# Pooled attention and a two-layer network on one core: the first four pairs of heads take fp32 products from TensorE

## The chip, the core and the metric

The kernel runs on one core of a Trainium2 chip. Five engines run side by side, each in the order of its own program: TensorE (PE, with its weight loads as PEld), VectorE (DVE), ScalarE (ACT), GpSimd (POOL) and SyncE (SP), which issues the DMAs. [...] The metric is the device time of one execution in microseconds; the profile's span runs from the first to the last instruction of one profiled execution.

## The reference

```python
q_pool = q.reshape(B, H, S // 2, 2, D).mean(axis=3)      # B, H, S, D = 4, 8, 1152, 64
scores = (1 / sqrt(D)) * q_pool @ k.T                      # 576 x 1152 per head
attn   = softmax(scores)                                   # over the 1152 keys
x      = (attn @ v) -> rows of 8 heads x 64 = 512          # 2304 rows
out    = (relu(x @ w_in) ** 2) @ w_out                     # 512 -> 2048 -> 512
```

All inputs and the output are fp32.

## The kernel before

Heads are worked on in 16 pairs, four for each batch. For a pair, `prep` loads K, Q and V (`LK`, `LQ`, `LV`), sums the two queries that are pooled (`QS`), finds a power of two as a scale for each (a maximum over sums of squares: ACT `Square` for pairs 0 and 5 to 15, TensorE products `GR` and `GM` for pairs 1 to 4, then the short chain `GF`, `GS`, `GT`, `GU`, `GW`), and splits each into two fp16 tensors, high and low (`KA`/`KD`, `QA`/`QD`, `VA`/`VD`). K and Q are then turned by DMA transposes (`KT`, `QT`), and `QX` copies the low half of Q to the other 64 partitions.

`chunk` handles 128 query rows, 9 chunks for a pair, 144 in all: scores `S` on TensorE (six fp16 matmuls), the row maximum `MX` on DVE, the exponential `EX` on ACT, which gives P in fp32. P goes on in one of two ways. Most chunks split it into high and low on ACT, POOL or DVE (`HI`, `LO`) and turn both by a DMA transpose (`TR`). The chunks of the list `TURNB` (16 of the first 36) are turned by TensorE: nine fp32 transposes in three groups (`TP`), each group in one of two PSUM banks, from which `TH` takes the high half and `TL` the rest. `group` then multiplies with V (`PV`): for each of 9 blocks of keys, three products (high by high, high by low, low by high) for each of two heads, whose 64 output rows lie beside each other, so 54 matmuls of 256 or 320 columns. `ED` scales the result into x.

`weights` brings in the two weight matrices in 16 pieces; each is taken apart and split by ACT, DVE and POOL (`W1` to `W5`, `WA`, `WB`, `WD`). `block` computes the network for 256 rows (9 blocks): after the sums (`RV`, `RB`, `XR`) and a split of x (`XA`, `XD`) come 192 matmuls `H` and 96 matmuls `O`, with `HA`, `G1`, `G2`, `G3` between. A block needs all four pairs of its batch, so the first `H` comes after the first four pairs; the other twelve pairs run between `H` and `O` of earlier blocks.

`add` only notes an operation with its engines' costs, what it depends on and the buffers it takes. `Plan.order` then lays all operations out in a model of the engines and takes, for an engine that comes free, the operation of smallest priority among those that can start soon; the priority is the position in the work plus an offset for the kind of operation (`CFG['off']`, and `off0` for the first part). What comes out is the order in which each engine's instructions are written. Two PSUM banks `a` serve `TP`, `PV`, `H`, `O` and the small products alike; the scores have two areas of three banks each, which become six banks `t` once the last scores are done.

Of the kernel before, what the change touches and what calls it, by code (L numbers as in the profile page):

```python
# [8 lines left out]
F32 = mybir.dt.float32  # L9
# [47 lines left out]
class Plan:  # L57
# [15 lines left out]
    def add(self, name, engs, deps, emit, at, take=None, give=None, after=()):  # L73

        kind = name[0]
        off, off0 = cfg("off", {}), cfg("off0", {})
        self.at[name] = len(self.ops)
        prio = cfg("nudge", {}).get(len(self.ops), 0.0) + at + off.get(kind, DEF.get(kind, 0.0)) + (off0.get(kind, 0.0) if at < self.early else 0.0)
        self.ops.append(
            dict(name=name, engs=dict(engs), deps=[d for d in deps if d], emit=emit, pos=at, prio=prio, take=take, give=give, after=after)  # L80
        )
# [120 lines left out]
ALT = {"W4": "D", "NP": "A", "ED": "D", "HI": "PD", "LO": "P", "KA": "P", "QA": "P", "QX": "P", "VA": "P", "XA": "", "WA": "", "WD": "", "HA": "D", "G2": "PD", "G3": "D", "XQ": "", "RU": "D"}  # L202
DEF = {
# [7 lines left out]
def kernel(  # L211
# [133 lines left out]

    def prep(n):
# [44 lines left out]
        qse = alt("QS", POOL=1400, DVE=640)  # L391
        if gram_:
# [14 lines left out]
            for i, nm in enumerate("kqv"):  # L407
                L = "L" + nm.upper()
                add(("GR", n, nm), {"PE": 560}, [(L, n)], lambda o, i=i, nm=nm: gram(o, i, nm), need, take=(("GR", n, nm), ("a",), 0))
                add(("GM", n, nm), {"DVE": 200}, [("GR", n, nm)], lambda o, i=i, nm=nm: gmax(o, i, nm), need, give=("GR", n, nm))  # L410
            add(("QS", n), qse, [("GR", n, "q")], qsum, need)
            fdep = [("GM", n, nm) for nm in "kqv"]
        else:
# [12 lines left out]
            add(("QS", n), qse, [("LQ", n)], qsum, need)  # L426
            add(("QK", n), {"ACT": 1200}, [("LK", n)], lambda o: sq(o, 0, "k"), need, take=ktake)
            add(("QV", n), {"ACT": 1200}, [("LV", n)] + oldv, lambda o: sq(o, 2, "v"), need)
            add(("QQ", n), {"ACT": 700}, [("QS", n)], lambda o: sq(o, 1, "q"), need, take=qtake)
# [40 lines left out]
        for w, i0, i1 in (("qk", 0, 2), ("v", 2, 3)):  # L470
            fd = [d for x, d in zip("kqv", fdep) if x in w]
# [48 lines left out]
        add(("KA", n), alt("KA", ACT=1170, POOL=1400), [("GW", n, "qk"), ("LK", n)] , ka, need, take=kt_)  # L520
        add(("KD", n), {"DVE": 1500}, [("KA", n)], kd, need, give=("k", n))
        add(("KT", n), {"SP": 3200}, [("KD", n)] + old, kt, need, give=("k2", n))
        add(("QA", n), alt("QA", ACT=600, POOL=700), [("GW", n, "qk"), ("QS", n)] , qa, need, take=qt_)
        add(("QD", n), {"DVE": 760}, [("QA", n)], qd, need, give=("q", n))
        add(("QT", n), {"SP": 1700}, [("QD", n)] + old, qt, need, give=("q2", n))
        add(("QX", n), alt("QX", DVE=1100, POOL=2500), [("QT", n)] + old, qx, need)
        add(("VA", n), alt("VA", ACT=1170, POOL=1400), [("GW", n, "v"), ("LV", n)] + oldv, va, need)
        add(("VD", n), {"DVE": 1480}, [("VA", n)], vd, need, give=("v", n))

    def done(c):  # L530
        if c in turned_b:
            return [("TL", c, x) for x in range(3)]
        return [("TL", c)] if c in turned else [("TR", c)]
# [6 lines left out]
    def chunk(i):  # L540
# [12 lines left out]
        def st3():  # L553
            return sts[i % 2].rearrange("p a b -> p (a b)")[:, :1152]

# [72 lines left out]
        ring = [("PV", v_, GR_[g_]) for v_, g_ in ring]  # L628
        if i in turned:
# [77 lines left out]
    def group(vi, r):  # L707
# [7 lines left out]
        def pv(o):  # L715
            vv = v2s[preps[n]["slot"]]
            px = bank(o)
            tl["px", vi, r] = px
            ps = [(vl, pl, kc) for vl, pl in ((1, 0), (0, 0), (0, 1)) for kc in range(NC)]
# [8 lines left out]
        def ed(o):  # L728
            px, sc = tl.pop(("px", vi, r)), tl["esc", n][:, 1:2]
# [4 lines left out]
        pc = 27 * (112 if N == TB else 138) + 100  # L734
# [3 lines left out]
        add(("PV", vi, r), {"PE": pc}, dn + [("VD", n)] + old, pv, last, take=(("PV", vi, r), ("a",), 0))  # L738
        add(("ED", vi, r), alt("ED", ACT=620 if r else 380, DVE=560 if r else 370), [("PV", vi, r), ("GE", n, "v")] + old,
# [397 lines left out]
    turned_b = {i for i in cfg("TURNB", range(0, FB, 4)) if CH[chunks[i][1]] is not None}  # L1137
# [12 lines left out]
    with tc.manual_schedule():  # L1150
# [7 lines left out]
        nc.vector.tensor_scalar(pick, pick, 2.0 ** -14, None, op0=ALU.mult)  # L1158
        for o in seq:
# [34 lines left out]
```

## Time and profile before

| what | value |
|---|---|
| time of three runs, median | 877.98 us (875.13 to 878.1) |
| span of the profiled execution | 873.5 us |
| what lies around the span, by the median | 4.5 us |
| busy in the span | PE 743.7, DVE 653.3, ACT 610.7, POOL 403.0 us |
| first matmul of the network (`H`) starts | 259.74 us |

The windows give busy microseconds and the granted TensorE clock of a stretch. A group of instructions lists the number, the busy time and the mean length in ns. In the timeline the first number is the start.

### The profile page before, as it was taken

How to read it: one execution, taken by the hardware profiler on the slowest of the kernel's cores; microseconds unless marked ns; L12 is line 12 of the kernel's file. 1: busy time of each engine (PE TensorE's matmuls, PEld its weight loads, DVE VectorE, ACT ScalarE, POOL GpSimd, SP SyncE). 2: the span in 40 equal slices, each digit the busy share in tenths (PEclk: the TensorE clock that was granted, in tenths of full speed). 3: DMA queues.
4: the chain of work that ended last, by engine and by line, in shares of the span. 5: the costliest groups of instructions: out<-in, count | busy, mean ns of one | idle time of the engine just before them, and what ended most of it. 6: DMA issues, size and time to landing. Idle time of an engine off the chain costs nothing. (4 is left out here: it accounts for less than half of the span.)

```text
span 873.5 us, 15476 instructions
## 1 busy us (share of the span) xinstructions
PE 743.7 (85%) x6041; PEld 495.6 (57%) x6041; DVE 653.3 (75%) x817; ACT 610.7 (70%) x959; POOL 403.0 (46%) x281
## 2 busy tenths in 40 slices
PE   0567656767579999998999999898999999999997
PEld 0344534544347567754775576566647756858573
DVE  4897999997878887988989788879788974312120
ACT  4666886778988778866896767777767984625150
POOL 2454436755878644555465266537835531100000
PEclk9976877799869999999999999999999999999999
DMA  7798796797668999989998989996889997000001
GB/s 220 223 176 210 163 245 179 184 220 150 134 144 156 174 160 201 164 182 184 173 195 150 197 159 172 204 179 141 153 183 181 183 158 133 2 13 13 13 14 24
DMA packets 346888, 133.39 MB, mean 153 GB/s; under 512 B 330176, under 2 KB 330176, under 8 KB 346816
## 3 DMA queue, kind: packets, MB, share of 16 engines
q1 hardware_dynamic: 346816, 132.41, 74.9%
q8 instruction: 47, 0.77, 0.4%
q14 instruction: 25, 0.20, 0.1%
HBM read 45.09 MB, written 4.72 MB: 57 GB/s over the span
## 5 line engine op out<-in xcount | busy, mean ns | idle before, releaser
L580 DVE TENSOR_REDUCE ca<-s 128x1 f32<-128x1152 f32 x144 | 192.6, 1348 | 13.5 <-PE s L572 8.9
L591 ACT ACTIVATE buf<-s,ca,esc 128x1152 f32<-128x1152 f32 x144 | 188.9, 1312 | 7.7 <-DMA PT<-buf 1.2
L603 POOL TENSOR_TENSOR buf<-buf,buf 128x1152 f16<-128x1152 f32 x60 | 152.6, 2545 | 88.2 <-ACT buf L595 61.9
L865 PEld LDWEIGHTS <-w 128*128 128x128 f16 x1728 | 168.7, 98 | 32.4 <-issue 8.3
L572 PE MATMUL s<-kT,qT 128*128 128x512 f16 (+1 forms) x768 | 156.9, 348 | 18.7 <-ACT buf L591 17.8
L914 PE MATMUL ba<-w,region 128*128 128x512 f16 x624 | 141.6, 379 | 0.7 <-DVE region L797 0.5
L914 PEld LDWEIGHTS <-region 128*128 128x128 f16 x864 | 82.9, 98 | 96.2 <-issue 2.9
L865 PE MATMUL ba<-region,w 128*128 128x256 f16 x1080 | 124.4, 274 | 6.3 <-DVE x L797 3.5
L572 PEld LDWEIGHTS <-qT 128*128 128x128 f16 x768 | 71.9, 105 | 86.1 <-issue 37.5
L723 PE MATMUL ba<-PT,v 128*64 128x256 f16 (+1 forms) x1728 | 116.0, 293 | 5.6 <-DVE PT L681 4.5
L723 PEld LDWEIGHTS <-v 128*64 128x64 f16 x1728 | 97.8, 113 | 22.5 <-issue 12.3
L603 DVE TENSOR_TENSOR buf<-buf,buf 128x1152 f16<-128x1152 f32 x56 | 84.6, 1510 | 14.6 <-ACT buf L595 12.3
L590 ACT ACTIVATE ca<-ca,cols,esc 128x1 f32<-128x1 f32 x144 | 54.6, 379 | 50.4 <-DVE ca L580 49.9
L892 DVE TENSOR_TENSOR region<-region 128x512 f16<-128x512 f32 x41 | 35.0, 854 | 63.0 <-ACT region L885 62.5
L658 PE MATMUL ba<-ident,buf 128*128 128x128 f32 x252 | 47.6, 312 | 35.2 <-DVE PT L681 14.7
L340 POOL TENSOR_SCALAR buf<-buf,cols 128x1152 f16<-128x1152 f32 x31 | 42.6, 1373 | 63.9 <-ACT buf L591 55.9
L595 ACT ACTIVATE buf<-buf 128x1152 f16<-128x1152 f32 x59 | 68.5, 1161 | 2.5 <-DVE buf L603 0.6
L343 DVE SCALAR_TENSOR_TENSOR buf<-raw,psc,buf 128x576 f16<-128x576 f32 x48 | 64.5, 1381 | 5.6 <-POOL buf L317 3.2
L658 PEld LDWEIGHTS ba<-ident,buf 128*128 128x128 f32 x252 | 31.3, 159 | 50.4 <-DVE PT L681 18.9
L892 POOL TENSOR_TENSOR region<-region 128x512 f16<-128x512 f32 x31 | 43.7, 1411 | 32.4 <-ACT region L885 29.5
L667 ACT ACTIVATE PT<-ba 128x384 f16<-128x384 f32 x84 | 39.2, 485 | 20.0 <-PE ba L658 19.4
L914 PE MATMUL bt<-w,region 128*128 128x512 f16 x240 | 52.9, 379 | 0.0
(135 smaller groups left out, 979.7 us busy)
## 6 DMA issues: line engine op xcount, KB each, us to landing
raw<-in_k_dram SPq DMA_DIRECT2D x16, 576.0 KB, 4.6
raw<-in_q_dram SPq DMA_DIRECT2D x32, 288.0 KB, 4.4
raw<-in_v_dram SPq DMA_DIRECT2D x16, 576.0 KB, 4.2
region<-in_moe_w_in_dram SPq DMA_DIRECT2D x8, 1024.0 KB, 5.8
region<-in_moe_w_out_dram SPq DMA_DIRECT2D x8, 1024.0 KB, 5.9
out_dram<-buf SPq DMA_DIRECT2D x36, 128.0 KB, 2.4
PT<-buf SPq DMA_TRANSPOSE x132, 4.8
qT<-buf SPq DMA_TRANSPOSE x32, 3.5
```

The source lines that it names most:

```text
L343: nc.vector.scalar_tensor_tensor(out=o, in0=x, scalar=s, in1=h, op0=ALU.mult, op1=ALU.subtract)
L572: nc.tensor.matmul(s[:, x, :w], lhsT=qt[:, l, h, c0 : c0 + 2, :].rearrange("p a b -> p (a b)"), rhs=rhs, **st)
L580: nc.vector.reduce_max(a[:, 0:1], st3(), axis=AX.X)
L590: nc.scalar.activation(a[:, 1:2], a[:, 0:1], AF.Identity, bias=ln14, scale=tl["esc", n][:, 0:1])
L591: nc.scalar.activation(P(), st3(), AF.Exp, bias=a[:, 1:2], scale=tl["esc", n][:, 2:3], accum_out=col)
L595: nc.scalar.activation(hl()[:, 0], P(), AF.Copy)
L603: e.tensor_tensor(out=hl()[:, 1], in0=P(), in1=hl()[:, 0], op=ALU.subtract)
L658: nc.tensor.matmul(t[:, y], lhsT=P()[:, c * 128 : (c + 1) * 128], rhs=ident, is_transpose=True, start=(y == 0), stop=False, skip_group_che ...
L723: nc.tensor.matmul(px[h * 64 : (h + 1) * 64, :N], lhsT=vv[:, h, kc, vl, :], rhs=t[:, 9 * pl + kc, :N], start=(i == 0), stop=(i == 3 * NC - ...
L865: nc.tensor.matmul(ph[:, f2], lhsT=w16[0][:, SLOT[f // 4], wl, a, f % 4 * 128 : (f % 4 + 1) * 128], rhs=xhl()[:, xl, a], start=(i == 0), s ...
L892: e.tensor_tensor(out=gt[u][:, 1], in0=rt[u % 2], in1=gt[u][:, 0], op=ALU.subtract)
L914: nc.tensor.matmul(p[:, :DM], lhsT=g[:, gl, f % 2, tt * 128 : (tt + 1) * 128], rhs=w16[1][:, SLOT[f // 4], wl, f % 4], start=(f == 0 and g ...
```

## The change

For the first four pairs V is loaded straight into its place as fp32 (`full_v`), with no scale and no split. All 36 chunks of these pairs are turned by TensorE, and each group of three transposes is copied once, in fp32, to `PT` (`TC`, by ACT or DVE); `PV` is one fp32 product for each block of keys, 18 matmuls in place of 54. For the first pair (`full_s`) K and Q are turned by fp32 matmuls against the identity (`KX`, `QY`), copied (`KC`, `QC`), and the scores are one fp32 product, three matmuls in place of six. `COST` replaces some costs in the model, and the offsets in `CFG` are all others, so that the order of the whole program differs. `TURNB` keeps only its chunks after the first 36.

```diff
-CFG = {...}
+CFG = {..., 'FS': (0,), 'FV': (0, 1, 2, 3)}
...
+COST = {
+    ("EX", "ACT"): 1710, ("RV", "DVE"): 1800, ("WS3", "DVE"): 1010, ("WS1", "DVE"): 456, ("HI", "ACT"): 1070,
...
+        if n in full_v:
+            add(("LV", n), {"SP": 2500}, oldv, lambda o: load_kv(v4(slot), v), need, after=[("LQ", n)])
...
+            def kx(o, x):
+                tl["kx", n, x] = t = bank(o, 3, 128)
+                for y in range(3):
+                    for h in range(2):
+                        nc.tensor.matmul(
+                            t[h * 64 : h * 64 + 64, y], lhsT=rk()[:, h, 3 * x + y, :], rhs=ident,
+                            start=True, stop=True, skip_group_check=True,
+                        )
...
+        def scores4(o):
+            s = sts[i % 2]
+            kt, qt = k4(slot), q4(slot)
+            for x in range(3):
...
+                nc.tensor.matmul(
+                    s[:, x, :w], lhsT=qt[hs, cs].rearrange("p a b -> p (a b)"),
+                    rhs=kt[hs, k0:k1].rearrange("p a b -> p (a b)"), start=True, stop=True,
+                )
...
+            def tc4(o, x):
+                t = tl.pop(("tp", i, x))
+                for y, p in enumerate(pts):
+                    o_, w = (256, 64) if CH[j] is None else (GRP[j][1], 128)
+                    out, src = p[:, 3 * x : 3 * x + 3, o_ : o_ + w], t[:, :, y * 64 : y * 64 + w]
+                    if o["eng"] == "ACT":
+                        nc.scalar.activation(out, src, AF.Copy)
+                    else:
+                        nc.vector.tensor_copy(out, src)
...
+            if n in full_v:
+                vv = v4(preps[n]["slot"])
+                for kc in range(NC):
+                    for h in range(2):
+                        t = p4(PTs[gidx[vi, gg[h]] % NPT])
+                        nc.tensor.matmul(
+                            px[h * 64 : (h + 1) * 64, :N], lhsT=vv[:, h, kc, :], rhs=t[:, kc, :N],
+                            start=(kc == 0), stop=(kc == NC - 1), skip_group_check=True,
+                        )
+                return
```

ACT at the start of the program. Before, its first work is the squares of K and Q, the high half of K, and two pieces of weights, and then the first exponential (L590, L591):

```order
L424 ACTIVATE buf_93,acc<-raw_100 128x1152
L424 ACTIVATE buf_94,acc<-raw_101 128x576
L315 ACTIVATE buf_93<-raw_100,psc 128x18x64
L973 ACTIVATE w_0_90<-region 128x1024
L978 ACTIVATE region<-region 128x1024
...
L424 ACTIVATE v_0_106,acc<-raw_101 128x18x64
L315 ACTIVATE v_0_106<-raw_101,psc 128x18x64
L590 ACTIVATE ca<-ca,cols,esc 128x1
L591 ACTIVATE buf_95,sums_85<-s_113,ca,esc 128x1152
```

Now it copies the turned K and Q out of PSUM (L421), takes one piece of weights, and comes to the first exponential (L689, L690):

```order
L421 ACTIVATE kT_102<-ba_115 128x384
L421 ACTIVATE kT_102<-ba_116 128x384
...
L421 ACTIVATE qT_104<-ba_116 128x320
L421 ACTIVATE qT_104<-ba_115 128x192
L421 ACTIVATE qT_104<-ba_115 64x64 x2
L1113 ACTIVATE w_0_90<-region 128x1024
L1118 ACTIVATE region<-region 128x1024
L689 ACTIVATE ca<-ca,cols 128x1
L690 ACTIVATE buf_93,sums_85<-s_113,ca 128x1152
```

The squares, the scale, the split of the first K, Q and V, and one piece of weights no longer stand ahead of the first exponential (the second of two pieces before, and now a third copy of K, are the rows left out).

DVE at the first chunks. Before, the maxima (L580) alternate with the rests of P taken from the banks (L681), a high half of P (L599) and the weights (L982, L986):

```order
L580 TENSOR_REDUCE ca<-s_113 128x1
L580 TENSOR_REDUCE ca<-s_114 128x1
L405 TENSOR_REDUCE acc<-ba_116 128x1
L599 CAST buf_97<-buf_96 128x1152
L681 TENSOR_TENSOR PT_108<-ba_115,PT_108 128x3x128
L681 TENSOR_TENSOR PT_108<-ba_116,PT_108 128x3x128
```

Now some of the copies of P (L752) stand there, beside the split of the second pair's K (L352) and the weights (L1122, L1126):

```order
L352 SCALAR_TENSOR_TENSOR buf_96<-raw_100,psc,buf_96 128x9x64 x2
L1122 TENSOR_SCALAR w_0_90<-w_0_90 128x1024
L752 COPY PT_108<-ba_116 128x3x128
L1126 SCALAR_TENSOR_TENSOR w_0_90<-region,w_0_90 128x1024
L752 COPY PT_108<-ba_115 128x3x128
L678 TENSOR_REDUCE ca<-s_113 128x1
```

DVE has no second pass over a bank there; the copies that it does not make are ACT's.

PE behind the first scores of the first pair. Before, a score is a run of weight loads and fp16 matmuls (L572); a group of three transposes (L658) stands between the products for a maximum (L401, L434) ahead of it:

```order
L401 LDWEIGHTS raw_101
L401 MATMUL ba_116<-raw_101 128x128
L658 MATMUL ba_115<-ident,buf_98 128x128 x3
L434 MATMUL ba_116<-acc,cols 128x2
L572 LDWEIGHTS qT_104
L572 MATMUL s_113<-kT_102,qT_104 128x512
```

Now three fp32 score matmuls (L649) alternate with such groups (L738):

```order
L649 MATMUL s_113<-kT_102,qT_104 128x512 x2
L649 MATMUL s_113<-kT_102,qT_104 128x128
L511 MATMUL ba_116<-acc,cols 128x2
L738 MATMUL ba_115<-ident,buf_93 128x128 x3
L649 MATMUL s_114<-kT_102,qT_104 128x512 x2
L649 MATMUL s_114<-kT_102,qT_104 128x128
L738 MATMUL ba_115<-ident,buf_93 128x128 x3
L738 MATMUL ba_116<-ident,buf_93 128x128 x3
```

Every chunk now sends three groups of transposes through PE and its two banks; before, every second one did.

In both kernels the same work stands on PE ahead of the first `H`: the scores of 46 chunks and 9 products with V. From the first `H` on, the kinds and numbers of matmuls are the same in both (1728 of `H`, 864 of `O`, 98 chunks of scores, 23 products with V, 99 transposes).

## Rows read from the trace of the kernel before

**Rows 1.** Windows: stretch, its length, busy PE, PEld, DVE, ACT, POOL; clock; DMA.

```profile
0.00:26.36 26.36, 5.44 (x32) 3.73 (x33) 13.01 (x27) 11.15 (x13) 7.71 (x13) 1.00 0.81 242
26.36:259.74 233.38, 149.46 (x1222) 98.36 (x1220) 206.78 (x269) 186.40 (x271) 139.93 (x82) 0.82 0.79 182
...
259.74:730.00 470.26, 450.23 (x3784) 301.24 (x3783) 400.82 (x465) 361.75 (x594) 251.68 (x177) 0.99 0.93 173
730.00:873.50 143.50, 138.59 (x1010) 92.27 (x1007) 32.64 (x59) 51.41 (x81) 3.66 (x10) 0.99 0.11 22
```

**Rows 2.** Chain that ended last, in order of time: start, us, what.

```profile
737.19 3.79 PE ba L723 x54
```

**Rows 3.** Timeline of the first 45 us: start, us, engine, line.

```profile
7.81 1.40 POOL L384 TENSOR_TENSOR raw<-raw 128x576 f32<-128x576 f32 x1 [6.50 <-DMA raw<-in_q_dram]
...
23.80 2.73 PE L572 MATMUL s<-kT,qT 128*128 128x512 f16 x12
...
26.36 2.61 DVE L580 TENSOR_REDUCE ca<-s 128x1 f32<-128x1152 f32 x2
```

**Rows 4.** Groups on DVE, 0 to 262 us: busy us, mean ns, idle before.

```profile
L681 DVE TENSOR_TENSOR PT<-ba,PT 128x384 f16<-128x384 f32 x51 | 27.0, 549 | 5.8 <-ACT PT L667 5.7
L343 DVE SCALAR_TENSOR_TENSOR buf<-raw,psc,buf 128x576 f16<-128x576 f32 x18 | 20.4, 1163 | 3.8 <-ACT buf L315 2.4 <-POOL buf L317 1.4
...
L343 DVE SCALAR_TENSOR_TENSOR v<-raw,psc,v 128x576 f16<-128x576 f32 x12 | 14.6, 1254 | 5.6 <-ACT v L315 5.6
L982 DVE TENSOR_SCALAR w<-w 128x1024 int32<-128x1024 int32 x12 | 13.8, 1151 | 0.4 <-ACT w L973 0.4
L603 DVE TENSOR_TENSOR buf<-buf,buf 128x1152 f16<-128x1152 f32 x6 | 8.3, 1392 | 0.3 <-ACT buf L595 0.3
...
L509 DVE COPY qT<-qT 64x1152 f16<-64x1152 f16 x4 | 4.5, 1134 | 0.1
L444 DVE TENSOR_SCALAR psc<-psc 128x2 int32<-128x2 int32 x6 | 4.4, 740 | 0.1
...
L982 DVE TENSOR_SCALAR region<-region 128x1024 int32<-128x1024 int32 x4 | 2.8, 709 | 0.6 <-ACT region L973 0.6
```

**Rows 5.** Groups on DVE that read PSUM, whole span.

```profile
L877 DVE TENSOR_SCALAR region<-ba 128x512 f32<-128x512 f32 x24 | 16.5, 688 | 13.9 <-PE ba L865 12.8 <-POOL region L892 1.1
...
L319 DVE TENSOR_SCALAR region<-ba,esc 128x256 f32<-128x256 f32 x5 | 2.4, 480 | 4.0 <-PE ba L723 4.0
...
L319 DVE TENSOR_SCALAR xm<-ba,esc 128x64 f32<-128x64 f32 x4 | 1.1, 275 | 0.0
```

**Rows 6.** Groups on ACT, 0 to 262 us.

```profile
L667 ACT ACTIVATE PT<-ba 128x384 f16<-128x384 f32 x51 | 23.7, 485 | 10.8 <-PE ba L658 10.2
...
L595 ACT ACTIVATE buf<-buf 128x1152 f16<-128x1152 f32 x14 | 16.3, 1161 | 0.4
```

**Rows 7.** Timeline of PE about three transposes, 292.5 to 296 us.

```profile
293.20 0.49 PE L658 MATMUL ba<-ident,buf 128*128 128x128 f32 x3
...
293.62 1.17 PE L567 MATMUL s<-kT,qT 128*64 128x512 f16 x12
```

**Rows 8.** Groups on PE, whole span.

```profile
L1020 PE MATMUL ba<-region 128*128 128x128 bf16 x32 | 2.3, 218 | 1.1 <-DVE wsc L1026 1.0
```

**Rows 9.** Line L1043 alone: min/median/max ns, first and last start.

```profile
L1043 PE MATMUL ba<-buf,cols x4: 275/326/376, 110.7 to 210.8; 128*128 128x128 f32 x4
```

**Rows 10.** Timeline of PE about one product with V, 307 to 312 us.

```profile
307.47 3.14 PE L723 MATMUL ba<-PT,v 128*64 128x256 f16 x54 [0.78 <-DVE psc L440]
307.47 2.87 PEld L723 LDWEIGHTS <-v 128*64 128x64 f16 x53 [0.75 <-issue]
...
310.54 1.15 PE L572 MATMUL s<-kT,qT 128*128 128x512 f16 x6
...
311.53 0.81 PE L914 MATMUL ba<-w,region 128*128 128x512 f16 x3
```

**Rows 11.** Waits, 0 to 260 us: us in total, times, longest.

```profile
PE ba L658 <- DVE PT L681: 14.5, 10, 4.5
```

More of the change, by code (lines that the diff above doesn't have):

```diff
@@ L78, in add @@
         prio = cfg("nudge", {}).get(len(self.ops), 0.0) + at + off.get(kind, DEF.get(kind, 0.0)) + (off0.get(kind, 0.0) if at < self.early else 0.0)
+        engs = {e: COST.get((kind, e), c) for e, c in engs.items()}
         self.ops.append(
[L80 removed]
+            dict(name=name, engs=engs, deps=[d for d in deps if d], emit=emit, pos=at, prio=prio, take=take, give=give, after=after)
         )
@@ L391, in prep, with move, kc, qy @@
         qse = alt("QS", POOL=1400, DVE=640)
+        todo = ("" if n in full_s else "kq") + ("" if n in full_v else "v")
+        if n in full_s:
+            kt4, qt4 = k4(slot), q4(slot)
+            def move(o, out, x):
+                if o["eng"] == "ACT":
+                    nc.scalar.activation(out, x, AF.Copy)
+                else:
+                    nc.vector.tensor_copy(out, x)
+            def kx(o, x):
[6 more added lines that the diff above has]
+                        )
+            def kc(o, x):
+                move(o, kt4[:, 3 * x : 3 * x + 3], tl.pop(("kx", n, x)))
+            def qy(o, z):
+                tl["qy", n, z] = t = bank(o, 5, 64)
+                for y in range(5 - z):
+                    for h in range(2):
+                        hs = slice(h * 64, h * 64 + 64)
+                        nc.tensor.matmul(t[hs, y], lhsT=rq()[:, 5 * z + y, 0, :], rhs=ident[:, hs], start=True, stop=True, skip_group_check=True)
+            def qc(o, z):
+                t = tl.pop(("qy", n, z))
+                if z == 0:
+                    move(o, qt4[:, :5], t)
+                else:
+                    move(o, qt4[:, 5:8], t[:, :3])
+                    for h in range(2):
+                        hs = slice(h * 64, h * 64 + 64)
+                        move(o, qt4[hs, 9 + h], t[hs, 3])
+            add(("QS", n), qse, [("LQ", n)], qsum, need)
+            for x in range(3):
+                add(("KX", n, x), {"PE": 750}, [("LK", n)] + old, lambda o, x=x: kx(o, x), need, take=(("KX", n, x), ("a",), 0), give=("k", n) if x == 2 else None)
+                add(("KC", n, x), alt("KC", ACT=380, DVE=460), [("KX", n, x)] + old, lambda o, x=x: kc(o, x), need, give=("KX", n, x))
+            for z in range(2):
+                add(("QY", n, z), {"PE": 1100 - 220 * z}, [("QS", n)] + old, lambda o, z=z: qy(o, z), need, take=(("QY", n, z), ("a",), 0), give=("q", n) if z else None)
+                add(("QC", n, z), alt("QC", ACT=350 + 350 * z, DVE=400 + 300 * z), [("QY", n, z)] + old, lambda o, z=z: qc(o, z), need, give=("QY", n, z))
@@ L519, in prep @@
         kt_, qt_ = (ktake, qtake) if gram_ else (None, None)
[L520 to L528, printed above, removed]
+        if "k" in todo:
+            add(("KA", n), alt("KA", ACT=1170, POOL=1400), [("GW", n, "qk"), ("LK", n)] , ka, need, take=kt_)
+            add(("KD", n), {"DVE": 1500}, [("KA", n)], kd, need, give=("k", n))
+            add(("KT", n), {"SP": 3200}, [("KD", n)] + old, kt, need, give=("k2", n))
+            add(("QA", n), alt("QA", ACT=600, POOL=700), [("GW", n, "qk"), ("QS", n)] , qa, need, take=qt_)
+            add(("QD", n), {"DVE": 760}, [("QA", n)], qd, need, give=("q", n))
+            add(("QT", n), {"SP": 1700}, [("QD", n)] + old, qt, need, give=("q2", n))
+            add(("QX", n), alt("QX", DVE=1100, POOL=2500), [("QT", n)] + old, qx, need)
+        if "v" in todo:
+            add(("VA", n), alt("VA", ACT=1170, POOL=1400), [("GW", n, "v"), ("LV", n)] + oldv, va, need)
+            add(("VD", n), {"DVE": 1480}, [("VA", n)], vd, need, give=("v", n))
     def done(c):
+        if chunks[c][0] in full_v:
+            return [("TC", c, x) for x in range(3)]
         if c in turned_b:
@@ L628, in chunk, with tp4 @@
         ring = [("PV", v_, GR_[g_]) for v_, g_ in ring]
+        if n in full_v:
+            pts = [p4(PTs[gidx[vi, g] % NPT]) for g in gs]
+            def tp4(o, x):
+                t = bank(o, 3, 128)
+                for y in range(3):
+                    c = 3 * x + y
+                    nc.tensor.matmul(
+                        t[:, y], lhsT=P()[:, c * 128 : (c + 1) * 128], rhs=ident, is_transpose=True,
+                        start=(y == 0), stop=(y == 2), skip_group_check=True,
+                    )
+                tl["tp", i, x] = t
+            def tc4(o, x):
[3 more added lines that the diff above has]
+                    out, src = p[:, 3 * x : 3 * x + 3, o_ : o_ + w], t[:, :, y * 64 : y * 64 + w]
+                    if o["eng"] == "ACT":
+                        nc.scalar.activation(out, src, AF.Copy)
+                    else:
+                        nc.vector.tensor_copy(out, src)
+            w = 240 if CH[j] is None else 0
+            for x in range(3):
+                add(("TP", i, x), {"PE": 440}, [("EX", i)] + ring + ([("TP", i, x - 1)] if x else []), lambda o, x=x: tp4(o, x), i, take=(("TP", i, x), ("a",), 0), give=("P", i) if x == 2 else None)
+                add(("TC", i, x), alt("TC", ACT=380 + w, DVE=460 + w), [("TP", i, x)] + ring, lambda o, x=x: tc4(o, x), i, give=("TP", i, x))
+            return
         if i in turned:
@@ L1136 @@
     plan.early = FB
-    turned_b = {i for i in cfg("TURNB", range(0, FB, 4)) if CH[chunks[i][1]] is not None}
+    full_s, full_v = set(cfg("FS", ())), set(cfg("FV", ()))
+    turned_b = {i for i in cfg("TURNB", range(0, FB, 4)) if CH[chunks[i][1]] is not None and chunks[i][0] not in full_v}
     turned = turned_b | {i for i in cfg("TURN", range(2, FB, 4)) if CH[chunks[i][1]] is not None}
@@ L1158 @@
         nc.vector.tensor_scalar(pick, pick, 2.0 ** -14, None, op0=ALU.mult)
+        for i in range(2):
+            nc.gpsimd.memset(q4(i)[:, 9:11], 0.0)
         for o in seq:
```

70 lines of the change are left out of this document (52 added, 18 removed), and 3 rows, old and new, of tables (COST, DEF).

## The prediction

> **What bounds the kernel now.** I read the windows first, cut where the first score maximum (26.36 us) and the first network matmul `H` (259.74 us) stand. They show three parts [rows 1]. [...] Ahead of it no engine is full: between 26.36 and 259.74 us DVE is busy for 206.8 of 233.4 us (88.6%), ACT for 186.4 (80%), PE for 149.5 (64%) at a mean clock of 0.82. DVE is the nearest to full there, and the groups of DVE then say with what: beside the score maxima, the second pass over the banks of turned P, and the splits of K, Q, V and P [rows 4]. Up to 26.36 us the first pair's scales, splits and transposes hold everything up; its first scores start at 23.80 us [rows 3].
>
> The order shows the same matmuls from the first `H` on in both kernels, so the later 614 us have the same work on the engine that bounds them. The question is thus when the first `H` can start. It needs x of all first four pairs, and its DVE program comes ahead of it in order: what DVE has to do up to the split of the first x is a bound.
>
> **The change on DVE, up to the first x.** Counts are those of the order, durations those of the rows.
> - Gone: 48 of 51 second passes over a bank, 48 x 0.549 = 26.4 us; 10 of 12 halves of V, 10 x 1.254 = 12.5; 4 of 6 low halves of P, 4 x 1.392 = 5.6; 3 of 18 halves of K and Q, 3 x 1.163 = 3.5 [rows 4]. Sum 48.0.
> - Added: six more copies of Q's low half, which POOL did, 6 x 1.134 = 6.8 [rows 4]; 39 copies of 384 columns and 8 of 192 out of PSUM. No such copy is in the trace. Reading PSUM, 64 columns took 0.275 us, 256 took 0.480, 512 took 0.688 [rows 5], so that 384 lie between 0.480 and 0.688 and 192 between 0.275 and 0.480. I take 0.55 (also the length of the two-operand pass over 384 columns [rows 4]) and 0.40: 39 x 0.55 + 8 x 0.40 = 24.7, with ends of 20.9 and 30.7.
> - Small: one chain of scales for K and Q and four for V fewer (the longest instruction of it 0.740 [rows 4]), three maxima and one high half fewer, two passes over weights that POOL takes: an estimate of 6 us less.
> - POOL gets rid of most of its low halves there. The same pass over weights took 1.151 us in twelve places and 0.709 in four [rows 4]; if the longer ones come from sharing with a busy POOL, up to 12 x 0.44 = 5.3 us go. I count 3, between nothing and all.
>
> DVE had 13.0 + 206.8 = 219.8 us [rows 1]; it keeps 219.8 - 48.0 + 31.5 - 6 - 3 = 194.3.
>
> **The start.** Now Q is in and summed at 7.81 + 1.40 = 9.2 us [rows 3], and K is turned by then. An fp32 matmul has two records in the trace; one of 128 columns takes at least 275 ns [rows 9] where a 16-bit one takes 218 [rows 8], so that each record holds one pass more, four in all. A pass over 128 columns is then 57 ns; six score matmuls of 2304 columns take 311.53 - 310.54 = 0.99 us [rows 10], 0.43 ns a column, which says the same. Turning Q: 18 matmuls of four passes over 64 columns, 2 us at the full clock, 4 at half of it. The copies of it: four on ACT at 0.3 to 0.5 us [rows 6], 1.6. A score: 4 x 1152 x 0.43 = 2.0 us, 4.0 at half. So the first maximum comes at 9.2 + 4 + 1.6 + 3 = 18 us, between 16 and 22, not 26.36. DVE has then done about 2 us and has 192 left. At the share of before, 192 / 0.886 = 217, and the first `H` is at 18 + 217 = 235 us, 25 earlier.
>
> **The other engines.** ACT loses 11 high halves, 11 x 1.161 = 12.8 us, and the squares, scales and splits of the first pair; it gains 9 copies of 0.485 and 16 of half their size [rows 6]: from 197.6 us [rows 1] to about 181, below DVE. PE gains, at the full clock: scores of nine chunks 9 x (2.0 - 0.99) = 9; 180 transposes at (293.62 - 293.20) / 3 = 0.14 us [rows 7], 25; turning K and Q, 3 to 8, say 5. A product with V has 36 passes in place of 27, if the two heads still run beside each other: before 307.47 to 310.54, 3.07 us for 256 columns [rows 10], and 3.79 for 320 [rows 2], now 4.1 and 5.05; eight products give 9. In all 47 us (27 fewer small products take 1.5 off). PE had 154.9 us at a mean clock of 0.84 [rows 1]. If the greater work brings the clock to 1.0, it has 130 + 47 = 177 us of 235, 75%; if the clock stays, 155 + 56 = 211, 90%. What hides the 47 us is thus PE's idle time, and the cover is thin. The transposes need the two banks. PE stood 14.5 us for a second pass [rows 11]; now a bank is free after one copy of 0.485 to 0.55, not after 0.485 + 0.549, but there are twice as many. What stands behind a waiting transpose on PE are the next scores, and DVE's maxima wait for these. I count these two against each other.
>
> On SP 20 transposes of P and the first pair's own go; DMA is no bound in that part.
>
> **Sum.** 873.5 - 25 = 848.5 us of span, with the 4.5 us that lie around it by the median (877.98 - 873.5) 853. I take 852, since the earlier start of the second pair's loads is not in the sum.
>
> [...]
>
> **Rivals.**
> 1. PE becomes the bound. If fp32 matmuls of the two heads run one behind the other, a product takes 18 x 4 x 256 x 0.43 = 7.9 us, or 9.9, eight of them 71 in place of 37, and PE has 211 to 251 us by the clock. At DVE's share of before it needs (211 to 251) / 0.886 from about 10 us on: the first `H` at 248 to 293, a time of 866 to 911, most likely 885. It decides once a product of 256 columns takes more than about 6.5 us. For it: two heads in fp32 are in no row. Against it: in fp16 they overlap fully.
> 2. The new order costs behind 259.74 us what the start gives. PE stood there for 25 of 614 us only [rows 1], which is all that a better order can find; a worse one has no such limit. If PE's busy share falls from 95.9% to 93%, 589 us need 633, 19 more: 871. For it: every offset is another. Against it: same work, same banks.
> 3. The stall goes further: the scores of the first pair no longer wait for scales, banks turn faster, and DVE is busy for 95%: 18 + 192 / 0.95 = 220, a time of 838; or the later part also gains 8: 830. For it: DVE is fed more evenly once POOL and the DMA transposes are off the way of P. Against it: PE, in its fixed order, has more to do ahead of each maximum.
>
> **Numbers.** Forecast 0.60, rival 1 0.14, rival 2 0.13, rival 3 0.13. The forecast's own range is 840 to 866: copies at their dearest and no relief by POOL, (192 + 9) / 0.886, put the first `H` at 245; the cheapest at 227; the rest is the later part, 4 us either way. What a measurement can tell from no change is 0.5%, 4.4 us, so faster is below 873.6 and slower above 882.4. Faster: 0.59 + 0.13 + 0.06 of rival 2 = 0.78; the same: 0.01 + 0.05 of rival 2 + 0.04 of rival 1 = 0.10; slower: 0.10 + 0.02 = 0.12. A range of 828 to 880 leaves out most of rival 1 and the far end of rival 3.
>
> **What would show it.** The first `H` at about 235 us, the first maximum at about 18; DVE near 194 us busy up to there; an fp32 product of 256 columns with V at 4.1 us, a copy of 384 columns on DVE at 0.55; PE's clock above 0.84 ahead of the first `H`; 614 us behind it. The prediction is wrong if PE waits on the banks for more than 30 us ahead of the first `H`, if a product with V takes 7 us or more, or if the part behind the first `H` is off by more than 10 us.

## The result, and the profile after

The changed kernel took 865.67 us (median of four runs, 861.94 to 869.06), the kernel before 877.34 on the same chip: a ratio of 0.9861, with an interval of 0.9823 to 0.9899. The gain is 1.4%; forecast were 852 us, 2.9%. The profiled execution took 867.78 us with a span of 866.0. The two profiled spans lie 7.5 us apart (873.5 and 866.0), the medians 11.7, so the windows below show some 4 us less of the gain than the medians do. In all that follows a time is the median of all runs of a kernel, and a ratio leaves out runs more than 1.5% above the fastest run of the same kernel.

Its windows, cut at the first score maximum and at the first network matmul `H` as in [rows 1] (length, busy time of PE, PEld, DVE, ACT, POOL, granted clock, DMA share, GB/s):

```profile
0.00:13.57 13.57, 8.14 (x79) 6.62 (x80) 1.25 (x8) 5.61 (x10) 2.39 (x9) 1.00 0.86 260
13.57:231.90 218.33, 183.23 (x1238) 113.55 (x1237) 186.05 (x249) 170.99 (x276) 86.98 (x53) 0.87 0.57 148
...
231.90:866.00 634.10, 595.44 (x4792) 397.03 (x4790) 442.24 (x527) 406.07 (x669) 284.04 (x199) 0.98 0.71 134
```

The part behind the first `H` in the kernel before, as one window:

```profile
259.74:873.50 613.76, 588.82 (x4792) 393.51 (x4790) 433.46 (x523) 413.16 (x675) 255.34 (x187) 0.99 0.74 138
```

The start gave 259.74 - 231.90 = 27.8 us. The later part took back 634.1 - 613.8 = 20.3, with the same 4792 records on PE: its idle time went from 24.9 to 38.7 us (13.7 more), its busy time from 588.8 to 595.4 (6.6 more) at a clock of 0.98, not 0.99.

The start, in the timeline (start, us, engine, line), answers to [rows 3], and the first `H`:

```profile
7.85 1.40 POOL L407 TENSOR_TENSOR raw<-raw 128x576 f32<-128x576 f32 x1 [6.26 <-DMA raw<-in_q_dram]
...
9.30 1.76 PE L442 MATMUL ba<-ident,raw 128*64 128x64 f32 x36
...
13.57 1.35 DVE L678 TENSOR_REDUCE ca<-s 128x1 f32<-128x1152 f32 x1
```

```profile
231.90 2.78 PE L1005 MATMUL ba<-buf,w 128*128 128x256 f16 x24
```

Groups on DVE up to 234 us (number, busy us, mean ns), against [rows 4]:

```profile
L752 DVE COPY PT<-ba 128x384 f32<-128x384 f32 x39 | 20.5, 548 | 7.9 <-PE ba L738 4.4 <-ACT xm L324 3.4
...
L1122 DVE TENSOR_SCALAR w<-w 128x1024 int32<-128x1024 int32 x12 | 10.7, 889 | 12.1 <-ACT w L1113 12.0
...
L352 DVE SCALAR_TENSOR_TENSOR v<-raw,psc,v 128x576 f16<-128x576 f32 x4 | 5.2, 1340 | 0.3 <-POOL v L326 0.3
...
L752 DVE COPY PT<-ba 128x192 f32<-128x192 f32 x8 | 2.4, 350 | 0.0
...
L811 DVE TENSOR_TENSOR PT<-ba,PT 128x384 f16<-128x384 f32 x3 | 1.7, 554 | 0.7 <-ACT PT L797 0.6
```

An fp32 product with V, in PE's timeline, against the 3.14 us of [rows 10]:

```profile
64.49 4.36 PE L854 MATMUL ba<-PT,v 128*64 128x256 f32 x36
```

PE's waits behind the first `H` (total us, times, longest), first after, then before:

```profile
PE s L670 <- ACT buf L690: 5.8, 8, 1.1
PE ba L788 <- DVE PT L811: 3.9, 6, 1.2
PE ba L788 <- DVE x L937: 3.5, 1, 3.5
PE ba L863 <- DVE PT L811: 3.2, 1, 3.2
PE ba L863 <- DVE buf L1068: 2.4, 2, 1.4
PE ba L902 <- DVE xm L328: 2.3, 1, 2.3
```

```profile
PE ba L865 <- DVE x L797: 3.5, 1, 3.5
PE ba L658 <- DVE buf L928: 2.5, 3, 1.2
PE ba L723 <- DVE PT L681: 2.4, 3, 1.2
PE s L572 <- ACT buf L591: 2.2, 5, 0.6
```

No single wait explains it; the longest is 3.5 us, as before. Much of what grew are short handovers: the scores waited 5.8 us in 8 places for an exponential (2.2 in 5 before), the turned banks 3.9 in 6 for the pass over the bank before them. A loss of that kind has no single line in a profile.

### The profile page after: what moved, and what is told of

The parts are those of the page before. It is cut to its first block, busy times and chain, and to the rows that moved or that the text cites. A ratio compares the mean times of both kernels' runs of the same rounds, so it can differ in the third digit from the quotient of the medians.

```text
span 866.0 us, 15480 instructions
## 1 busy us (share of the span) xinstructions
PE 786.8 (91%) x6106; PEld 517.2 (60%) x6106; DVE 629.5 (73%) x782; ACT 582.7 (67%) x953; POOL 373.4 (43%) x261
## 5 line engine op out<-in xcount | busy, mean ns | idle before, releaser
L690 ACT ACTIVATE buf<-s,ca,esc 128x1152 f32<-128x1152 f32 x135 | 177.0, 1311 | 6.9 <-POOL buf L702 0.3
L702 POOL TENSOR_TENSOR buf<-buf,buf 128x1152 f16<-128x1152 f32 x55 | 139.2, 2534 | 58.5 <-ACT buf L694 35.6
L1054 PE MATMUL ba<-w,region 128*128 128x512 f16 x672 | 153.3, 382 | 1.0 <-ACT ru L908 1.0
L670 PE MATMUL s<-kT,qT 128*128 128x512 f16 x720 | 138.9, 333 | 10.5 <-ACT buf L690 10.3
L863 PE MATMUL ba<-PT,v 128*64 128x320 f16 (+1 forms) x1296 | 88.5, 296 | 6.3 <-DVE PT L811 3.2
L863 PEld LDWEIGHTS <-v 128*64 128x64 f16 x1296 | 74.6, 114 | 19.8 <-issue 12.6
L689 ACT ACTIVATE ca<-ca,cols,esc 128x1 f32<-128x1 f32 x135 | 51.4, 381 | 50.1 <-DVE ca L678 49.8
L702 DVE TENSOR_TENSOR buf<-buf,buf 128x1152 f16<-128x1152 f32 x41 | 64.7, 1578 | 9.6 <-ACT buf L694 5.9
L738 PE MATMUL ba<-ident,buf 128*128 128x128 f32 x324 | 56.8, 306 | 16.2 <-DVE PT L752 8.0
L352 DVE SCALAR_TENSOR_TENSOR buf<-raw,psc,buf 128x576 f16<-128x576 f32 x45 | 55.7, 1272 | 3.4 <-POOL buf L326 3.4
L738 PEld LDWEIGHTS ba<-ident,buf 128*128 128x128 f32 x324 | 37.8, 153 | 33.5 <-DVE PT L752 13.7
L750 ACT ACTIVATE PT<-ba 128x384 f32<-128x384 f32 (+1 forms) x73 | 31.1, 454 | 27.5 <-PE ba L738 27.0
L1005 PE MATMUL bt<-region,w 128*128 128x256 f16 x432 | 49.2, 273 | 0.0
L1135 POOL TENSOR_TENSOR w<-w,region 128x1024 f32<-128x1024 f32 x11 | 26.5, 2410 | 52.2 <-DVE w L1126 50.0
```

The source lines that it names most:

```text
L352: nc.vector.scalar_tensor_tensor(out=o, in0=x, scalar=s, in1=h, op0=ALU.mult, op1=ALU.subtract)
L670: nc.tensor.matmul(s[:, x, :w], lhsT=qt[:, l, h, c0 : c0 + 2, :].rearrange("p a b -> p (a b)"), rhs=rhs, **st)
L702: e.tensor_tensor(out=hl()[:, 1], in0=P(), in1=hl()[:, 0], op=ALU.subtract)
L738: nc.tensor.matmul(t[:, y], lhsT=P()[:, c * 128 : (c + 1) * 128], rhs=ident, is_transpose=True, start=(y == 0), stop=(y == 2), skip_group_ ...
L863: nc.tensor.matmul(px[h * 64 : (h + 1) * 64, :N], lhsT=vv[:, h, kc, vl, :], rhs=t[:, 9 * pl + kc, :N], start=(i == 0), stop=(i == 3 * NC - ...
L1005: nc.tensor.matmul(ph[:, f2], lhsT=w16[0][:, SLOT[f // 4], wl, a, f % 4 * 128 : (f % 4 + 1) * 128], rhs=xhl()[:, xl, a], start=(i == 0), s ...
```

## The experiments

Each kernel shows its time, the ratio to the kernel before on the same chip, and the window behind its first `H`, which starts where the window starts. Each window is from one profiled execution.

**The numbers or the program.** Three kernels, run together, with the kernel before at 876.74 us. The first lays the changed program out with the offsets and costs of before:

```diff
-CFG = {..., 'FS': (0,), 'FV': (0, 1, 2, 3)}
+CFG = {...as before..., 'FS': (0,), 'FV': (0, 1, 2, 3)}
-COST = {
...
+COST = {}
```

> The changed program (fp32 parts as they are) under the order's numbers of before: all offsets, slacks and weights of CFG, no COST. Theory A (the 20 us lost behind the first H are the new numbers' doing): the part behind the first H takes 614 us, within 8, as before; the first H comes somewhat later than 232 us, 235 to 255, since these numbers were not made for the changed start; time 855 to 872. Theory B (they belong to the changed program: with a shorter start less other work is done ahead, and the later part has more of it, whatever the order): that part takes 628 us or more.

881.66 us, ratio 1.0048 (1.0021 to 1.0074):

```profile
230.88:878.60 647.72, 600.83 (x4792) 399.19 (x4790) 430.25 (x526) 413.60 (x673) 247.81 (x184) 0.97 0.69 130
```

The second lays out the program of before with the new numbers:

```diff
-CFG = {..., 'FS': (0,), 'FV': (0, 1, 2, 3)}
+CFG = {..., 'FS': (), 'FV': ()}
```

> The program of before (no fp32 part, no pair in FS or FV, the same list of turned chunks as before) under the new numbers. Theory A: the part behind the first H takes 628 us or more, so that the time is above 885. Theory B: 614 us, within 8. The first H should come at 260 us or later by both.

921.3 us, ratio 1.0516 (1.0481 to 1.0552). Here four chunks of scores and a product more lay behind the first `H`:

```profile
265.40:922.50 657.10, 611.85 (x4882) 405.61 (x4881) 441.98 (x556) 425.88 (x684) 247.93 (x181) 0.97 0.71 132
```

The third leaves out the fp32 scores of the first pair alone:

```diff
-CFG = {..., 'FS': (0,), 'FV': (0, 1, 2, 3)}
+CFG = {..., 'FS': (), 'FV': (0, 1, 2, 3)}
```

> The changed program with the first pair's scores in fp16 as before (K, Q scaled, split and turned by DMA), everything else as in the change, new numbers. If the fp32 scores of the first pair are worth the earlier first maximum (13.6 us against 26.4): 8 to 12 us slower than the change, first H at 240 to 244. If the cold PE (fp32 scores at half the clock up to 56 us) eats that: within 3 us of the change. The part behind the first H should stay near 634 by theory A and B.

883.58 us, ratio 1.0086 (1.0057 to 1.0116):

```profile
235.84:879.30 643.46, 597.84 (x4792) 399.32 (x4790) 441.10 (x535) 411.18 (x671) 247.01 (x180) 0.98 0.69 131
```

Without these scores the start lost 3.9 us (235.84 against 231.90), not 8 to 12, and the later part, laid out differently again, 9.4 more. With 18 us above the changed kernel the time was a miss for both readings. Nor were the changed kernel's fp32 scores all at half the clock up to 56 us: four of the nine took 4.21 us, the last of them ending at 55.7, the other five 2.1 to 3.2.

Neither theory holds as it was put. Most of the early gain belongs to the program: its first `H` comes at 231 with either set of numbers. With the old ones PE's clock was 1.00 from 20 to 40 us (18.47 us busy), with the new ones 0.56; in an execution with 1.00 there the new ones have the `H` at 221.7, as the last section shows, so that by these single executions some 9 us are theirs. But the later part takes 614 us only in the kernel before, and 634 to 657 in the four others, three of which have the same 4792 records on PE. The change on its old numbers is 0.5% slower than no change; the numbers found anew brought 16 us of that back.

**Old numbers for the later part alone:**

```diff
+        if at >= self.early:
+            off, off0 = OLD["off"], {}
...
+            if o["name"][0] == "H" and o["pos"] == self.early:
+                slack = {x: OLD["sl" + x] for x in self.SLACK}
+                pen, bl = OLD["pen"], OLD["bl"]
...
-        at = FB + cfg("MSP", 16) * m
+        at = FB + OLD["MSP"] * m
```

> The changed program; operations that stand ahead of the first network block keep the new numbers, those at or behind it get the offsets of before, and the slacks of before hold from the first H on. Theory A: first H at 225 to 240 us, 614 us behind it, time 844 to 858. Theory B: 628 us or more behind it, time about 866.

888.78 us by the median of all ten runs (877.21 to 894.55), ratio 1.0084 (1.0046 to 1.0123), a miss:

```profile
252.05:891.90 639.85, 596.17 (x4802) 397.83 (x4801) 453.57 (x538) 412.84 (x676) 265.01 (x192) 0.98 0.72 135
```

The profiled execution took 893.67 us. The edit did not keep the start either: the first `H` was expected at 225 to 240 and came at 252.05, and 4802 records stand behind it, not 4792. An order is not carried over by its numbers; with half of them exchanged, the planner laid out something else on both sides of the first `H`.

**The order itself.** So the written list was carried over. Behind the first `H` the planner's list is replaced by a list of names and engines, read from another kernel's plan; an operation is taken once its inputs stand ahead of it and a buffer is free.

```diff
-    seq = plan.order(("EX", NSTEP - 1))
+    seq = relay(plan, plan.order(("EX", NSTEP - 1)), LATE, NBUF, NRAW, NSTEP)
...
+        for k, (x, e) in enumerate(todo):
+            o = rest[x]
+            if any(d not in done for d in list(o["deps"]) + list(o["after"])):
+                continue
```

> The changed kernel up to the first H, word for word; behind it the kernel before's order: on every engine the same operations in the order, and on the engine, that they have there (what the kernel before had done ahead of its first H and this one not - a low half, its transposed load, a Q load and its sum - comes first). Theory C, the time of the later part goes with the exact order in which its operations stand, which was found together with that kernel's own start: first H at 232, the part behind it 614 (608 to 622), 850 us in all, 16 below the changed kernel. Theory D, the later part is slower because of what the changed start leaves (DMA and queues in another phase, buffers, the clock), whatever the order: first H at 232, behind it 634 (628 to 645), 866 to 875 in all.

862.36 us, ratio 0.9853 (0.9812 to 0.9894):

```profile
233.20:865.10 631.90, 594.48 (x4792) 395.53 (x4790) 434.65 (x529) 413.76 (x676) 258.31 (x190) 0.98 0.72 134
233.20:273.20 40.00, 30.02 (x254) 23.34 (x252) 24.17 (x30) 23.46 (x39) 23.58 (x18) 0.87 0.65 117
```

> The mirror image: the kernel before up to its first H, word for word; behind it the changed kernel's order. Theory C: first H at 260, the part behind it 634 (628 to 645), 898 us in all. Theory D: the part behind it stays at 614 (608 to 622), 878 in all. If an order runs well only behind the start for which it was found, this kernel and the one with the changed start and the order before both come out above 625 behind the first H.

895.27 us, ratio 1.0216 (1.0183 to 1.0249):

```profile
260.70:894.40 633.70, 594.92 (x4792) 396.99 (x4790) 437.97 (x521) 404.92 (x668) 281.60 (x197) 0.98 0.71 133
```

The mirror image speaks for theory C: the changed kernel's list takes 633.7 us behind the old start too, where it takes 634.1 behind its own. It does not lose them where the lists meet: in the first 40 us PE is busy for 37.32 (before 39.34, changed 37.93), and far behind, from 400 to 500 us after the first `H`, its busy time follows the changed kernel's, here in the kernel before, the changed one and the mirror image:

```profile
659.74:759.74 100.00, 97.18 (x900) 68.63 (x898) 71.65 (x95) 75.50 (x123) 36.00 (x29) 1.00 0.77 134
631.90:731.90 100.00, 91.05 (x797) 60.56 (x797) 79.99 (x92) 69.01 (x114) 50.40 (x33) 1.00 0.90 159
660.70:760.70 100.00, 91.51 (x798) 60.75 (x798) 78.51 (x92) 69.72 (x116) 49.41 (x33) 1.00 0.90 161
```

The first of the two looked like D. But its loss lies in one place. The product with V that began 47.7 us behind the first `H` in the kernel before [rows 10] begins 60.1 behind it here:

```profile
293.30 3.14 PE L1101 MATMUL ba<-PT,v 128*64 128x256 f16 x54 [0.73 <-DVE psc L755]
```

12.4 of the 18.1 us are lost by then, most of them in one wait, which the timelines of DVE, SP, POOL, ACT and PE show as a chain:

```profile
233.31 3.65 DVE L590 SCALAR_TENSOR_TENSOR v<-raw,psc,v 128x576 f16<-128x576 f32 x2
```

```profile
237.02 1.12 SPq L632 DMA_DIRECT2D raw<-in_q_dram  x2
```

```profile
243.07 1.40 POOL L645 TENSOR_TENSOR raw<-raw 128x576 f32<-128x576 f32 x1 [6.73 <-DMA raw<-in_q_dram]
```

```profile
247.17 0.67 ACT L736 ACTIVATE buf<-raw 128x576 bf16<-128x576 f32 x1
```

```profile
247.99 0.59 PE L749 MATMUL ba<-acc,cols 128*128 128x2 f32 x2 [7.80 <-ACT buf L736]
```

The split of v holds a raw buffer until 237; only then is the next q loaded, and its sum, its norm and PE's matmul of the norm follow. The old list has that load long behind it when it comes to this matmul. So most of this kernel's loss is at the seam between two orders, not in the later part.

**The seam mended.** The norm, scales and split of v of that prep, and the load and sum of q of the next, are moved up the list, so that all of them stand well ahead of the first `H`. The kernel holds the whole list; what changed in it is given here in short, as moves of one operation to the place behind another:

```diff
+move(('QV',5),('XN',0))
+move(('GF',5,'v'),('RB',1,0))
...
+move(('VA',5),('WD',1,3))
+move(('VD',5),('XM',0))
+move(('LQ',6),('TR',38))
+move(('QS',6),('XU',0))
```

> The kernel with the changed start and the order before behind it (862.36, first H at 233.2, 631.9 behind it) loses 12.4 of its 18 us within 60 us of its first H: TensorE stands 7.80 us for the norms of the sixth prep, whose q load was issued only after that H, because its raw buffer was held by the split of v of the prep before; the granted clock falls to 0.87 for the 40 us. Here that norm, split, load and sum (QV, GF to GW, VA, VD of prep 5, then LQ and QS of prep 6) stand some 60 operations earlier, ahead of the first H; all else is the same order. If that seam is the loss: first H at 231 to 236, no such wait behind it, the part behind it 616 to 622, 852 to 858 in all, under both the changed kernel (865.67) and the one before. If the time behind the first H is set by something else in the changed program, it stays at 628 to 636, and the time at 860 to 868.

860.23 us, ratio 0.9781 (0.9723 to 0.9839):

```profile
240.20:860.30 620.10, 590.53 (x4792) 393.26 (x4790) 427.64 (x527) 413.53 (x676) 254.26 (x189) 0.99 0.74 136
```

The part behind the `H` came out as expected, the time did not: the wait now stood ahead of the `H`, which came 7 us later.

```profile
218.60 2.13 PE L914 MATMUL s<-kT,qT 128*64 128x512 f16 x12 [4.24 <-ACT buf L939]
...
230.94 0.90 PE L1037 MATMUL ba<-ident,buf 128*128 128x128 f32 x3 [5.66 <-DVE xs L593]
```

So the same operations were moved less far:

```diff
-move(('GF',5,'v'),('RB',1,0))
-move(('VD',5),('XM',0))
-move(('LQ',6),('TR',38))
+move(('GF',5,'v'),('LO',38))
...
+move(('VD',5),('HI',41))
+move(('LQ',6),('TH',40,1))
...
```

> In the kernel with the mended seam (860.23) the part behind the first H took 620.1, as expected, but the first H came at 240.2 instead of 233.2: ahead of it TensorE waits 4.24 us for an exponential and 5.66 for the norm of the first output block, since the moved operations stood before their inputs were there and held DVE's and ACT's queues. Here the same operations are moved by about 10 us of work instead of 15, the split of v behind the first block's own chain. If the two parts are separate: first H at 233 to 237, behind it 617 to 624, 851 to 860 in all. If the work ahead of the first H can't be had for less (what the start gains by leaving it, the later part pays): first H plus the rest stays at 860 to 865.

853.22 us (848.16 to 857.13), ratio 0.9716 (0.9658 to 0.9774): under the kernel before and the changed one. The windows, and the same product with V, which now begins 284.68 - 237.0 = 47.7 us behind the first `H`, as in the kernel before:

```profile
237.00:855.20 618.20, 589.88 (x4792) 392.68 (x4790) 430.91 (x524) 413.19 (x675) 257.42 (x189) 0.99 0.73 136
237.00:277.00 40.00, 39.25 (x333) 29.19 (x332) 33.38 (x38) 31.64 (x54) 29.85 (x22) 0.99 0.87 157
```

```profile
284.68 3.14 PE L1112 MATMUL ba<-PT,v 128*64 128x256 f16 x54 [0.25 <-DVE psc L766]
```

With the seam closed, the changed start and the old list give what theory C said: 608 to 622 us behind the first `H`, 850 in all. Theory D falls.

**Positions or engines.** The two lists differ in the sequence and in the engine that an operation was given. Each was combined with the other's half. In each case 200 operations of the list change engine and none its place; in the first kernel, for instance:

```diff
-    ... (('HI', 44), 'ACT'), (('S', 46), 'PE'), ...
+    ... (('HI', 44), 'DVE'), (('S', 46), 'PE'), ...
```

> The changed kernel (865.67, 634.1 behind the first H); behind the first H its own sequence is kept, but each operation that may run on several engines runs on the engine that the kernel before gave it (47 low halves of P, 50 high halves and some 100 others change place). If the 16 us between the two later parts (634 and 618) lie in the engines chosen: 616 to 624 behind the first H, 850 to 858 in all. If they lie in the positions: 630 to 640, 862 to 874. If position and engine fit each other only as a pair, it is worse than either: above 640, above 874.

890.98 us, ratio 1.0166 (1.0103 to 1.0228), with 47 low halves of P, 50 high halves and some 100 others on another engine:

```profile
20.00:40.00 20.00, 17.32 (x85) 10.31 (x85) 17.78 (x26) 16.75 (x28) 7.18 (x6) 1.00 0.79 213
221.70:884.70 663.00, 601.18 (x4792) 399.56 (x4789) 427.43 (x529) 411.85 (x676) 250.41 (x190) 0.98 0.67 128
```

> The other half of the table: the best kernel so far (853.22, first H at 237, 618.2 behind it, the order before there), with the changed kernel's engines for the operations behind the first H. If the engines decide: 630 to 640 behind the first H, 868 to 880 in all. If the positions decide: 616 to 624, 851 to 858. If they fit only as a pair: above 640, above 880.

885.28 us, ratio 1.0108 (1.0071 to 1.0144):

```profile
20.00:40.00 20.00, 17.32 (x83) 10.21 (x83) 17.48 (x25) 16.38 (x28) 7.54 (x7) 0.97 0.80 225
230.00:879.80 649.80, 599.95 (x4792) 397.37 (x4790) 426.07 (x525) 403.50 (x669) 270.33 (x198) 0.98 0.69 130
```

Both are worse than either whole, 663 and 650 us against 634 and 618: the third outcome. Here sequence and engines fit only as a pair, so neither half of the new list can be named as its fault. Which of its places cost most stays open.

## Why the prediction failed

**The start: right, and in part by luck.** The first `H` came at 231.9, predicted 235; the first maximum at 13.57, predicted 18 (16 to 22, so early by more than its range). The prediction had costed Q's turn at half of the full clock, 4 us (the kernel before shows 0.50 from 60 to 70 us), and the scores at 3, between the 2.0 of the full clock and the 4.0 of half of it; Q's turn took 1.76 us and the clock was 1.00 up to 13.57 us. DVE was busy for 187.3 us up to the first `H` (1.25 + 186.05), predicted 194.3. Its copies took 0.548 us for 384 columns and 0.350 for 192, counted at 0.55 and 0.40. The twelve passes over weights went from 1.151 to 0.889 us, 12 x 0.26 = 3.1 us, counted as 3; the pass behind each of them went from 1.672 to 1.277, 4.7 us that the sum did not have. That POOL's lighter load did this is not shown. The waits on the banks did about cancel: PE's transposes waited 12.3 us for the copies out of a bank (8.0 for DVE, 4.3 for ACT), far from the 30 that would have made the prediction wrong, where they had waited 14.5 for the second pass.

DVE's share behind the first maximum was 85%, not 88.6%. This goes with PE's clock in the profiled execution, which was 0.51 on the mean between 18 and 38 us (last section). The kernel with the engines of before has the same order up to its first `H`, and its profiled execution shows 1.00 from 20 to 40 us and 0.92 in all:

```profile
13.57:221.65 208.08, 173.75 (x1238) 108.78 (x1237) 186.21 (x249) 171.19 (x276) 87.20 (x53) 0.92 0.59 155
```

There DVE's share is 89.5% and the first `H` comes at 221.7, ahead of the predicted 227 to 245. So in the execution compared here the lower clock took back 10 of the 13 us that the sum had counted too much, if the clock is all that differs between the two executions. Rival 3's share of 95% came in neither.

**Rival 1: false.** A product took 4.36 us, predicted 4.1; one head behind the other would have taken 7.9 by the prediction's estimate. So the fp32 heads ran beside each other here. PE was busy for 191.4 us ahead of the first `H` (8.14 + 183.23), within 177 to 211, and from 13.57 us on the clock there was 0.87, above the 0.84 asked for.

**The later part: the step that failed.** "The later 614 us have the same work on the engine that bounds them" is true of the work: PE is the engine meant, busy there for 588.82 of 613.76 us before, with 4792 records in both kernels. It was then used as if the time followed from the work: the range gave that part 4 us either way, and the rule for being wrong was set at 10; it was off by 20.3. The 25 us in which PE stood in the kernel before were taken for granted, but they were an achievement of one order. In every kernel here with another order behind the first `H` PE stood 38 us or more, at a clock of 0.97 or 0.98; with the old list and the seam closed it stood 28.3 us, at 0.99. Rival 2 had the mechanism, more waits of PE in a new order, and nearly the size (a third of it was busy time at a slightly lower clock, 6.6 us, which the rival did not have): it put PE's busy share at 93% and 633 us, which would give 871; measured were 93.9% (595.44 of 634.10) and 634.1. Its chance, 0.13, was too small. What the prediction gave against it, "same work, same banks", bears on the work and not on the waits. For it spoke that every offset had changed, and that a part at 96% busy can lose far more than it can gain.

**The sum.** In the profiled execution the start is 3.1 us better than predicted and the later part 20.3 worse: 17.2 of the 17.5 us between the predicted span, 848.5, and 866.0. The other difference is a slip: the 4.5 us around the span mixed the median of the runs with the span of one execution. In the changed kernel's profiled execution they are 867.78 - 866.0 = 1.8.

**The test of it.** With the old order behind the new start and the seam closed, the kernel takes 853.22 us (237.0 and 618.2 in its profile, predicted 235 and 614). The prediction of 852 was one for that kernel, not for the one with an order found anew.

## What to carry to other kernels

Where a planner lays out the whole program, a local change is two changes. Cost the part that it does not touch too: where an engine hardly stands there, expect a new order to give some of that back. Here every new one did, some 20 us and more. If a good order exists for the part that stays, carry over the written list and mend the seam, by looking for the one wait behind it and for what holds the buffer that it needs. Moving the numbers that once made the list does not carry it.

## What the runs showed of the hardware

PE was busy without a gap and yet at half of the full clock. In the changed kernel between 20 and 40 us it was busy for 20.00 of 20.00 us at a mean clock of 0.56 (0.50 from 20 to 36, for 16.00 of 16.00 us):

```profile
20.00:40.00 20.00, 20.00 (x51) 10.90 (x50) 9.69 (x14) 9.71 (x16) 5.23 (x6) 0.56 0.48 131
```

```profile
17.97 1.12 PE L472 MATMUL ba<-raw 128*128 128x128 bf16 x9 [2.07 <-DMA raw<-in_q_dram]
19.02 4.21 PE L649 MATMUL s<-kT,qT 64*128 64x512 f32 x6
...
30.02 4.21 PE L649 MATMUL s<-kT,qT 64*128 64x512 f32 x6
```

It stood 2.07 us for the load of q just before. The kernel with the engines of before has the same order up to its first `H`; in its profiled execution it stood 1.10 us for that load, and the same chunk of fp32 scores took 2.20 us, not 4.21:

```profile
17.03 0.68 PE L712 MATMUL ba<-raw 128*128 128x128 bf16 x9 [1.10 <-DMA raw<-in_q_dram]
17.64 2.20 PE L889 MATMUL s<-kT,qT 64*128 64x512 f32 x6
```

Its window from 20 to 40 us shows a clock of 1.00 and its `H` comes at 221.7, not 231.9. The same holds for the pair that shares the mended seam: 0.97 and 230.0 against 0.59 and 237.0. So one start has two outcomes, 7 to 10 us apart. What decides between them stays open: the length of a wait alone does not, since in the changed kernel a wait of 1.51 us that ended at 46.10 was followed by 0.50 from 48.10 to 56, and one of 2.25 us that ended at 703.77 by 1.00 up to 711.77, both with PE busy without a gap in these stretches. The four runs of the best kernel, 857.01, 848.16, 857.13 and 849.42 us, fall apart by as much, and their mean clocks go with it, 0.964, 0.972, 0.964 and 0.967; that this is the cause is argued, since only one of them has a profile. In the changed kernel the clock was 0.83 in the wait of 2.07 us that ended at 17.97 and 0.50 from there to 37.00, while PE was busy for 19.03 of 19.03 us.
